# Two interleaved streams of matrix products on one core: runs of second products in place of single ones

## The chip, the core and the metric

The kernel runs on one core of one Trainium2 chip. The metric is device time in microseconds; before the change the median of three runs is 1249.38 us (1248.95 to 1249.69). Engines are named as in the profile: PE is the matrix engine, PEld its weight load, DVE the vector engine, ACT the scalar engine, POOL the GpSimd engine, SP the engine that issues DMAs.

## What is computed

A block-sparse attention (4 batches, 8 heads, 768 tokens, head size 64) feeds a mixture of four dense experts over all 3072 tokens, each with a hidden layer of 1024:

```python
attn = softmax(mask(q @ k.T / 8)) @ v          # mask: window, first and last block, 3 sampled blocks
x = attn.transpose(0, 2, 1, 3).reshape(3072, 512)
p = domain_probs / domain_probs.sum(-1)
for e in range(4):
    h = relu(x @ w1[e])                        # 512 -> 1024: the "first" product
    out += p[:, e:e+1] * (h @ w2[e])           # 1024 -> 512: the "second" product
```

## The kernel before, in words

The expert layers take most of the time, and PE does them as two interleaved streams of work.

A **first product** (line 746, or 725 in the first two sets; written F here) is six matmuls of 128x384: a high part and a low part of weights and tokens (hi*hi, lo*hi, hi*lo) for two slices of 256 inputs, with 384 tokens as columns. In the last three of the five sets seven such products (numbered 2, 1, 5, 6, 3, 7, 4, in that order) stand in for eight, so that their sums are combined on ACT and DVE. Products 2, 5 and 3 are written to the PSUM tile `v`, the others are summed in the PSUM tile `w`; each tile has one buffer, so that a reader on ACT or DVE (`p`, `u`, `z`, `hh`, `hl` at lines 753 to 781) has to be done before PE writes it again. ACT then makes `hh` (ReLU, rounded), and DVE `hl` (the rest).

A **second product** (line 795, written S here) is three matmuls of 128x512 (hh*h2, hh*l2, hl*h2) for one tile of 128 tokens. Three token tiles j = 0, 1, 2 make up 384 tokens; four hidden tiles f = 0 to 3 are summed in the PSUM tile `po`, one buffer for each j. After f = 3 DVE adds `po` times the token's weight to `oacc` (line 810; the "evacuation"), and then f = 0 of the next group may write that buffer.

The function `experts` sets the order of the two streams by counting. It is a generator that emits one product at a time: p counts the first products that are out, q the second ones. Second product q becomes due when p has reached `lead[q]`, which spreads the second products evenly over the first ones at a distance of 10 (`OFF`). Each set of the last three has 8 chunks of 14 first and 24 second products; each of the first two sets has 8 chunks of 8 and 12. One more rule (`wait`) puts a second product ahead of first product 4, since 7 and 4 write `w` one after the other with a reader between them. With every first product the casts of a later weight tile are emitted as well: a copy on ACT (line 674), a difference on POOL (line 675), and, for 2, 1, 5 and 6, a sum or difference of raw weights on DVE (lines 678 to 684). `split_w2` (lines 698 and 699) does the same for `w2` after the last use of a tile.

The attention of the next batch is laid between the products by `drive`, which goes by the modelled time of what has been emitted: blocks of score matmuls (L347, L480), transposes (L385, L502) and value products (L416, L531), some of them only right after a second product (`drive(..., 2)`). All engines' queues are in program order. The order is fixed when the program is built.

Of the kernel before, what the change touches and what calls it, by code (L numbers as in the profile page):

```python
# [23 lines left out]
def attention_moe_kernel(ctx: ExitStack, tc, qb, kb, vr, sampled, sampled_t, probs, w1, w2, out):  # L24
# [193 lines left out]
    one = const.tile([1, 1], F32, name="one")  # L218
# [8 lines left out]
    lead = p1.tile([NR, G], F32, name="lead")  # L227
# [392 lines left out]
    def convert(b, r):  # L620
        if b in todo and todo[b][0][0] <= r:
            step(b)

    def need(b, n):
        while b in todo and any(m == n for _, _, m in todo[b]):
            step(b)
# [5 lines left out]
    def plain(m):  # L632
        return m < 2
# [80 lines left out]
    def first(b, c, s, n):  # L714
        ps_m, cp, hp = later["m"], later["c"], later["h"]
        w = wo.pop((b, c, s, n))
        if plain(b):
# [10 lines left out]
            if k == 1:  # L728
                f = 2 * s + i
                ring = int((c * FT + f + FT) % (NH[0] + NH[1]) >= NH[0])  # L730
                hh = hp.tile([P, HS], F32R, name=f"hh{ring}", bufs=NH[ring])
                hl = hp.tile([P, HS], F32R, name=f"hl{ring}", bufs=NH[ring])
                src = W[s]
# [16 lines left out]
        def finish(half, g, src):  # L750
            hh = hp.tile([P, HS], F32R, name=f"hh{g}", bufs=NH[g])
            hl = hp.tile([P, HS], F32R, name=f"hl{g}", bufs=NH[g])
            nc.scalar.activation(hh, src, AF.Relu)
            defer.append(lambda: nc.vector.scalar_tensor_tensor(hl, src, 0.0, f32(hh), op0=ALU.max,  # L754
                                                                op1=ALU.subtract))
            hs[c, 2 * s + half, g] = (hh, hl)
# [30 lines left out]
    def second(b, c, g, f, j):  # L787
        e = c // CPE
        if f == 0:
            po[j] = later["m"].tile([P, DM], F32, name="po", bufs=HS // P)  # L790
        p = po[j]
        (hh, hl), (h2, l2) = hs[c, f, g], w2t[b, c, f]
        js = slice(j * P, (j + 1) * P)
        for n, (a, w) in enumerate(((hh, h2), (hh, l2), (hl, h2))):
            nc.tensor.matmul(p, a[:, js], w, start=f == 0 and n == 0,  # L795
                             stop=f == FT - 1 and n == 2)
        if j == HS // P - 1:
            hs.pop((c, f, g))
            if g == 0 or plain(b):
                w2t.pop((b, c, f))  # L800
                split_w2((b * NCH + c + 1) * FT + f)
        if f < FT - 1:
            return
        tok = (b * HS if plain(b) else (b - 1) * S + g * HS) // P + j
        pe = pr[:, tok, e:e + 1]
        if c == 0:
            accs[tok] = later["o"].tile([P, DM], F32, name="oacc")
            nc.vector.tensor_scalar(accs[tok], p, pe, None, op0=ALU.mult)
        else:
            nc.vector.scalar_tensor_tensor(accs[tok], p, pe, accs[tok], op0=ALU.mult, op1=ALU.add)  # L810
        if c == NCH - 1:
            acc, row = accs.pop(tok), tok * P
            if b < 2:
                row += BLOCK
                if row + P > S:
                    nc.sync.dma_start(out[:BLOCK, :], acc[S - row:, :])
                nc.sync.dma_start(out[row:min(row + P, S), :], acc[:min(P, S - row), :])
            else:
                nc.sync.dma_start(out[row:row + P, :], acc)
# [2 lines left out]
    TB = NCH * (len(ORDER) * T1 + KT * FT * T2)  # L822
    TP = NCH * (len(PLAIN) * T1 + KT // 2 * FT * T2)
    OFF = 10
    NH = (5, 3)

    def experts():

        sets = []
        ends = [0]  # L830
        for b in range(SETS):
            sets.append(([(b, c, s, n) for c in range(NCH) for s, n in (PLAIN if plain(b) else ORDER)],
                         [(b, c, g, f, j) for c in range(NCH) for g in ((0,) if plain(b) else (1, 0))
                          for f in range(FT) for j in range(HS // P)]))
            ends.append(ends[-1] + len(sets[-1][0]))
        one = [x for a, _ in sets for x in a]
        two = [x for _, a in sets for x in a]

        lead = [ends[b] + i * len(a) / len(t) + OFF for b, (a, t) in enumerate(sets) for i in range(len(t))]

        def ready(p):

            q = 0
            for b, (a, t) in enumerate(sets):
                q += min(max(p - OFF + 1 - ends[b], 0), len(a)) * len(t) // len(a)
            return q

        p = q = 0
        after_first = False
        while q < len(two):  # L850

            left = defer[:]
            defer.clear()
            wait = after_first and p < len(one) and one[p][3] == 4 and q < ready(p)
            if wait or p >= min(len(one), lead[q]):
                second(*two[q])
                q += 1
                after_first = False
                took = T2, 2
            else:  # L860
                need(one[p][0], one[p][3])
                first(*one[p])
                p += 1
                after_first = True
                took = T1, 1
            for op in left:
                op()
            for b in todo:
                if p - ends[b] >= EARLY:
                    convert(b, p - ends[b])  # L870
                    break
            yield took

    stream = experts()
    done = [0.0]

# [238 lines left out]
```

## Time and profile before

| | us |
|---|---|
| median of three runs | 1249.38 |
| the profiled execution's own time | 1256.33 |
| its span, first to last instruction | 1254.6 |
| PE busy | 1228.3 (98%) |
| DVE busy | 759.5 (61%) |
| ACT busy | 675.6 (54%) |
| POOL busy | 715.1 (57%) |
| granted clock of PE, mean over the span | 0.997 |

The profiled execution is 7 us longer than the median. PE's busy time uses ends that are modelled, and a matmul's record overlaps the next one's; the distance from one start to the next is what tells the cost of a matmul here, so the timeline of PE's starts is the view to read. Rows of the timeline give start, duration, engine, line, operation and tiles; matmuls of one name in a row are merged with their count.

### The profile page before, as it was taken

How to read it: one execution, taken by the hardware profiler on the slowest of the kernel's cores; microseconds unless marked ns; L12 is line 12 of the kernel's file. 1: busy time of each engine (PE TensorE's matmuls, PEld its weight loads, DVE VectorE, ACT ScalarE, POOL GpSimd, SP SyncE). 2: the span in 40 equal slices, each digit the busy share in tenths (PEclk: the TensorE clock that was granted, in tenths of full speed). 3: DMA queues.
4: the chain of work that ended last, by engine and by line, in shares of the span. 5: the costliest groups of instructions: out<-in, count | busy, mean ns of one | idle time of the engine just before them, and what ended most of it. 6: DMA issues, size and time to landing. Idle time of an engine off the chain costs nothing.

```text
span 1254.6 us, 29430 instructions
## 1 busy us (share of the span) xinstructions
PE 1228.3 (98%) x11028; PEld 1051.0 (84%) x11028; DVE 759.5 (61%) x1743; ACT 675.6 (54%) x1817; POOL 715.1 (57%) x846
## 2 busy tenths in 40 slices
PE   5899999999999999999999999999999999999998
PEld 3688888878888888888888888888888888888887
DVE  5455536545448676656658676666756855555553
ACT  4556645666656446666665445666664544444441
POOL 5566656666659646555546664556544855555551
PEclk9899999999999999999999999999999999999999
DMA  8556646585635425444413442444431222222211
GB/s 242 159 184 172 192 167 214 181 233 183 189 104 196 152 77 153 151 126 124 131 60 131 160 125 84 138 153 135 142 91 47 89 97 66 67 70 68 66 51 54
DMA packets 75051, 163.84 MB, mean 131 GB/s; under 512 B 8923, under 2 KB 20188, under 8 KB 74908
## 3 DMA queue, kind: packets, MB, share of 16 engines
q1 hardware_dynamic: 69238, 144.65, 36.8%
q0 software_dynamic: 5632, 17.31, 5.0%
q8 instruction: 87, 1.43, 0.5%
q14 instruction: 56, 0.46, 0.1%
q10 hardware_dynamic: 38, 0.00, 0.0%
HBM read 155.63 MB, written 6.29 MB: 129 GB/s over the span
## 4 chain that ended last, share of the span: by engine, by line
PE 67%; DVE 2%; issue 0%; POOL 0%; POOLq 0%; DVEq 0%
PE po L795 32%; PE w L746 16%; PE v L746 12%; PE s L347 2%; PE o L416 2%; PE tp L385 1%; DVE oacc L810 1%; PE ow L531 1%; PE sw L480 1%; PE tw L502 0%; DVE d L597 0%; DVE hl L754 0%; DVE r L682 0%; PE w L725 0%; PE v L725 0%
## 5 line engine op out<-in xcount | busy, mean ns | idle before, releaser
L675 POOL TENSOR_TENSOR wo<-r,wo 128x256 fp32r<-128x256 f32 x288 | 241.2, 840 | 278.5 <-ACT wo L674 275.0
L795 PE MATMUL po<-h,hh 128*128 128x512 f32 x768 | 307.4, 400 | 1.4 <-DVE oacc L810 1.4
L795 PE MATMUL po<-h,hl 128*128 128x512 f32 x768 | 304.5, 397 | 0.0
L795 PE MATMUL po<-l,hh 128*128 128x512 f32 x768 | 303.5, 395 | 0.1
L746 PE MATMUL w<-xo,wo 128*128 128x384 f32 x1152 | 233.2, 337 | 0.2 <-DVE u L776 0.2
L699 POOL TENSOR_TENSOR l<-r,h 128x512 fp32r<-128x512 f32 x160 | 211.2, 1320 | 37.6 <-ACT h L698 36.9
L746 PEld LDWEIGHTS w<-xo,wo 128*128 128x128 f32 x1152 | 205.4, 188 | 19.2 <-DVE z L781 0.8
L746 PE MATMUL v<-xo,wo 128*128 128x384 f32 x864 | 176.1, 338 | 0.0
L795 PEld LDWEIGHTS po<-h,hl 128*128 128x128 f32 x768 | 143.8, 187 | 31.6 <-issue 0.3
L746 PEld LDWEIGHTS v<-xo,wo 128*128 128x128 f32 x864 | 154.6, 188 | 13.0 <-ACT z L773 0.2
L661 POOL TENSOR_TENSOR wo<-r,wo 128x256 fp32r<-128x256 f32 x128 | 95.8, 750 | 116.4 <-ACT wo L660 109.2
L795 PEld LDWEIGHTS po<-h,hh 128*128 128x128 f32 x768 | 144.2, 188 | 20.4 <-DVE oacc L810 2.8
L795 PEld LDWEIGHTS po<-l,hh 128*128 128x128 f32 x768 | 144.2, 188 | 12.4
L674 ACT CAST wo<-r 128x256 fp32r<-128x256 f32 x288 | 114.3, 397 | 49.1 <-PE w L746 31.3
L810 DVE SCALAR_TENSOR_TENSOR oacc<-po,pr,oacc 128x512 f32<-128x512 f32 x168 | 124.1, 741 | 24.1 <-PE po L795 24.0
L374 ACT ACTIVATE p<-p,mx 128x256 f32<-128x256 f32 (+1 forms) x192 | 95.4, 498 | 69.6 <-DVE mx L371 69.6
L698 ACT CAST h<-r 128x512 fp32r<-128x512 f32 x160 | 99.0, 619 | 11.5 <-PE po L795 11.3
L212 POOL DMA_INDIRECT v<-in_vr_dram,vidx x88 | 85.1, 967 | 26.6 <-issue 18.4
L371 DVE CUSTOM_DVE_ANT_1 p<-s,mask 128x256 f32<-128x256 f32 (+1 forms) x192 | 69.8, 418 | 49.1 <-PE s L347 38.6
L725 PE MATMUL w<-xo,wo 128*128 128x384 f32 x384 | 80.5, 342 | 1.1 <-issue 1.0
L725 PE MATMUL v<-xo,wo 128*128 128x384 f32 x384 | 78.4, 340 | 0.5 <-ACT xo L322 0.5
L769 DVE TENSOR_TENSOR p<-w,p 128x384 f32<-128x384 f32 x48 | 26.7, 555 | 84.8 <-PE w L746 81.6
(148 smaller groups left out, 1666.7 us busy)
## 6 DMA issues: line engine op xcount, KB each, us to landing
r<-in_w_dram SPq DMA_DIRECT2D x80, 512.0 KB
r<-in_w_dram SPq DMA_DIRECT2D x160, 256.0 KB
v<-in_vr_dram SPq DMA_DIRECT2D x44, 384.0 KB
kr<-in_kb_dram SPq DMA_DIRECT2D x76, 192.0 KB
k<-in_kb_dram SPq DMA_DIRECT2D x8, 768.0 KB
v<-in_vr_dram SPq DMA_DIRECT2D x12, 512.0 KB
out_dram<-oacc SPq DMA_DIRECT2D x23, 256.0 KB
q<-in_qb_dram SPq DMA_DIRECT2D x20, 256.0 KB
```

Of the source, the lines that this page charges most:

```text
L212: nc.gpsimd.indirect_dma_start(out=v[:G, i, 1], out_offset=None, in_=vr, element_offset=b * S * DM, in_offset=bass.IndirectOffsetOnAxis(ap ...
L371: nc.vector.tensor_tensor_reduce(p.rearrange("p (a b) -> p a b", b=BLOCK), s[h][:n, i], mk, -SCALE, 3.0e38, ALU.add, ALU.min, mx[:n])
L374: nc.scalar.activation(p, p, AF.Exp, bias=mx[:n], scale=-1.0, accum_out=self.sums[:n, m:m + 1])
L661: nc.gpsimd.tensor_sub(o[:, 1], r[s][:, i, k], f32(o[:, 0]))
L674: nc.scalar.copy(o[:, 0], src)
L675: nc.gpsimd.tensor_sub(o[:, 1], src, f32(o[:, 0]))
L698: nc.scalar.copy(h, r)
L699: nc.gpsimd.tensor_sub(l, r, f32(h))
L725: nc.tensor.matmul(W[s], w[:, wi, t], x[xi][:, k * KH + t], start=k == 0 and m == 0, stop=k == 1 and m == 3 * KH - 1)
L746: nc.tensor.matmul(ps, w[:, wi, t], x[:, xi, t], start=fresh and m == 0, stop=m == 3 * KH - 1, skip_group_check=not fresh)
L795: nc.tensor.matmul(p, a[:, js], w, start=f == 0 and n == 0, stop=f == FT - 1 and n == 2)
L810: nc.vector.scalar_tensor_tensor(accs[tok], p, pe, accs[tok], op0=ALU.mult, op1=ALU.add)
```

## The change

The loop in `experts` is given a counter `burst`. Where no run is under way, it looks whether the next three second products are all due (`RUN = 3`; fewer at the very end); if so it begins a run of them. If they are not, and the next first product is 4 and the last one was a first product, it begins a run of those that become due with that product, three at most. During a run only second products are emitted.

```diff
+    RUN = 3
...
-        p = q = 0
+        p = q = burst = 0
         after_first = False
         while q < len(two):
             left = defer[:]
             defer.clear()
-            wait = after_first and p < len(one) and one[p][3] == 4 and q < ready(p)
-            if wait or p >= min(len(one), lead[q]):
+            if not burst:
+                due = sum(1 for n in range(q, min(q + RUN, len(two))) if p >= min(len(one), lead[n]))
+                if due == min(RUN, len(two) - q):
+                    burst = due
+                elif after_first and p < len(one) and one[p][3] == 4:
+                    burst = min(RUN, ready(p) - q)
+            if burst:
+                burst -= 1
                 second(*two[q])
                 q += 1
                 after_first = False
```

The number of instructions is the same. In the built program, apart from the last 18 second products, which stand in a row in both, the 750 others stood in 158 runs of one and 296 runs of two, with one first product between two runs. They now stand in 250 runs of three, with one first product (48 times) or two (202 times) between them. The first run begins after 12 first products in place of 10. A run of three is j = 0, 1, 2 of one hidden tile.

PE in the last but one chunk of the last set, from first product 1 up to 6, around the second products f = 3 of the group `hh1`, whose results are evacuated. Before (`xo1`, `xo5`, `xo6` are the tokens' side of products 1, 5 and 6; `po` has one number for each j):

```order
L746 MATMUL w_16182<-xo1_14205,wo_16046 128x384 x6
L795 MATMUL po_16082<-h2_16075,hh1_16131 128x512
L795 MATMUL po_16082<-l2_16076,hh1_16131 128x512
L795 MATMUL po_16082<-h2_16075,hl1_16132 128x512
L795 MATMUL po_16098<-h2_16075,hh1_16131 128x512
L795 MATMUL po_16098<-l2_16076,hh1_16131 128x512
L795 MATMUL po_16098<-h2_16075,hl1_16132 128x512
L746 MATMUL v_16206<-xo5_14234,wo_16068 128x384 x6
L795 MATMUL po_16116<-h2_16075,hh1_16131 128x512
L795 MATMUL po_16116<-l2_16076,hh1_16131 128x512
L795 MATMUL po_16116<-h2_16075,hl1_16132 128x512
```

PE at the same place after the change:

```order
L746 MATMUL w_16182<-xo1_14201,wo_16046 128x384 x6
L746 MATMUL v_16197<-xo5_14230,wo_16059 128x384 x6
L795 MATMUL po_16108<-h2_16075,hh1_16128 128x512
L795 MATMUL po_16108<-l2_16076,hh1_16128 128x512
L795 MATMUL po_16108<-h2_16075,hl1_16129 128x512
L795 MATMUL po_16113<-h2_16075,hh1_16128 128x512
L795 MATMUL po_16113<-l2_16076,hh1_16128 128x512
L795 MATMUL po_16113<-h2_16075,hl1_16129 128x512
L795 MATMUL po_16117<-h2_16075,hh1_16128 128x512
L795 MATMUL po_16117<-l2_16076,hh1_16128 128x512
L795 MATMUL po_16117<-h2_16075,hl1_16129 128x512
```

First product 5 has moved ahead of the second products for j = 0 and 1; after them 6 and 3 follow as a pair, and then f = 0, j = 0 of the next group.

DVE at this place, from the sum of product 1 (`p`) to that of product 6 (`u`). Before:

```order
L769 TENSOR_TENSOR p_16169<-w,p_16169 128x384
L680 TENSOR_TENSOR r_16003<-r_16003 128x256
L810 SCALAR_TENSOR_TENSOR oacc<-po,pr,oacc 128x512
L754 SCALAR_TENSOR_TENSOR hl_16191<-p_16169,hh_16190 128x384
L810 SCALAR_TENSOR_TENSOR oacc<-po,pr,oacc 128x512
L682 TENSOR_TENSOR r_16003<-s_16171,r_16003 128x256
L810 SCALAR_TENSOR_TENSOR oacc<-po,pr,oacc 128x512
L776 TENSOR_TENSOR u_16233<-w,z_16213 128x384
```

After:

```order
L769 TENSOR_TENSOR p_16165<-w,p_16165 128x384
L680 TENSOR_TENSOR r_16003<-r_16003 128x256
L682 TENSOR_TENSOR r_16003<-s_16167,r_16003 128x256
L754 SCALAR_TENSOR_TENSOR hl_16191<-p_16165,hh_16190 128x384
L810 SCALAR_TENSOR_TENSOR oacc<-po,pr,oacc 128x512 x3
L776 TENSOR_TENSOR u_16229<-w,z_16204 128x384
```

The three evacuations now stand in one piece, all of them behind the weight difference of line 682 (which waits for POOL) and behind `hl`; before, only the third stood behind line 682.

## Prediction

> **What bounds the kernel now.** I read the page first, then the chain of work that ended last, then PE's waits, and then the timeline of PE's starts. In the page, the span and PE's row; of the chain, its shares by engine; of PE's waits, the only one that lies in the stream of products and exceeds a microsecond:
>
> ```profile
> span 1254.6 us, 29430 instructions
> PE 1228.3 (98%) x11028; PEld 1051.0 (84%) x11028; DVE 759.5 (61%) x1743; ACT 675.6 (54%) x1817; POOL 715.1 (57%) x846
> ...
> PE 67%; DVE 2%; issue 0%; POOL 0%; POOLq 0%; DVEq 0%
> ...
> PE po L795 <- DVE oacc L810: 1.4, 3, 0.5
> ```
>
> PE is busy 98% of the span, the chain runs through it, and it waits for others hardly at all. So the time is the sum of the distances between PE's starts, and a change in the order of products is worth what it changes in these distances, less any wait that it makes. The next view is PE's timeline in the last set, which has no attention; each row below opens a product or a run (second products have three rows each, only the first is shown).
>
> ```profile
> 1115.96 1.21 PE L746 MATMUL w<-xo,wo 128*128 128x384 f32 x6
> 1117.00 0.39 PE L795 MATMUL po<-h,hh 128*128 128x512 f32 x1
> ...
> 1118.39 1.21 PE L746 MATMUL v<-xo,wo 128*128 128x384 f32 x6
> 1119.43 0.39 PE L795 MATMUL po<-h,hh 128*128 128x512 f32 x1
> ...
> 1121.87 0.39 PE L795 MATMUL po<-h,hh 128*128 128x512 f32 x1
> ...
> 1122.57 1.22 PE L746 MATMUL v<-xo,wo 128*128 128x384 f32 x6
> 1123.63 0.39 PE L795 MATMUL po<-h,hh 128*128 128x512 f32 x1
> ...
> 1147.33 1.21 PE L746 MATMUL w<-xo,wo 128*128 128x384 f32 x6
> ```
>
> From 1115.96 to 1147.33 is one chunk, 14 first and 24 second products: 31.37 us. Inside it a run of two S takes 1118.39 - 1117.00 = 1.39, and the F behind it 1.04 (1119.43 - 1118.39). A single S takes 1122.57 - 1121.87 = 0.70, and the F behind it 1.06 (1123.63 - 1122.57). With 10 runs of two and 4 of one, and 1.045 for the F behind a run of two, this gives 10 x 2.435 + 4 x 1.76 = 31.39: the pieces account for the chunk.
>
> Now the same products where nothing alternates: the last second products of the program, behind the last F, and the first F of the program.
>
> ```profile
> 1237.26 1.21 PE L746 MATMUL w<-xo,wo 128*128 128x384 f32 x6
> 1238.30 0.39 PE L795 MATMUL po<-h,hh 128*128 128x512 f32 x1
> ...
> 1239.00 0.39 PE L795 MATMUL po<-h,hh 128*128 128x512 f32 x1
> ...
> 1239.69 0.39 PE L795 MATMUL po<-h,hh 128*128 128x512 f32 x1
> ...
> 1240.38 0.39 PE L795 MATMUL po<-h,hh 128*128 128x512 f32 x1
> ...
> 1249.22 0.39 PE L795 MATMUL po<-h,hh 128*128 128x512 f32 x1
> ```
>
> ```profile
> 54.93 2.24 PE L725 MATMUL w<-xo,wo 128*128 128x384 f32 x12
> 57.01 2.24 PE L725 MATMUL v<-xo,wo 128*128 128x384 f32 x12
> ...
> 63.25 0.39 PE L795 MATMUL po<-h,hh 128*128 128x512 f32 x1
> ```
>
> Behind an F, three S take 0.70, 0.69 and 0.69, 2.08 in all (1238.30 to 1240.38). The 13 S from 1240.38 to 1249.22 take 0.680 each. Eight F in a row (54.93 to 63.25) take 1.040 each. So an S that follows an F soon costs 0.01 to 0.02 more than one in a long row, and an F behind a single S 0.02 more than one behind an F. Alternating costs a little at every turn. That is the cost which longer runs can lower.
>
> **The change, part by part.** No instruction is added or removed; 454 runs of S become 250.
>
> The products themselves. In a chunk of the last three sets, 8 runs of three and 14 F: 8 x 2.08 + 14 x 1.04 = 31.20, against 31.37: 0.17 less, and for 24 such chunks 4.1. In a chunk of the first two sets, 4 runs of one and 4 of two become 4 of three, with 8 F: before 4 x 1.76 + 4 x 2.435 = 16.78, after 4 x 2.08 + 8 x 1.04 = 16.64: 0.14 less, and for 16 chunks 2.2. Together 6.3. In 8% of the runs an attention block stands at the edge (231 of the 250 runs follow an F directly), so I take 92%: **-5.8 us**.
>
> Two values in this are not shown by the trace as such. The third S of a run that an F follows: at least 0.68 (the long row), at most 0.70 (a single S); I take 0.69, the one third S there is. Over 250 runs that is 2.5 either way. The F behind a run of three: at least 1.04 (behind an F), at most 1.06 (behind a single S); it falls from 1.06 to 1.045 with the second S, so I take 1.04. The high end adds 0.02 x 250 = 5.0. All low ends give 0.92 x (-6.3 - 2.5) = -8.1; all high ends 0.92 x (-6.3 + 7.5) = +1.1.
>
> The Trainium skill, on the page "TensorE: Matmul & The Clock Gate", section "Back-to-back issue gap", gives the distance of matmuls from their own columns alone, N/2.4 + 2.5 ns; by it the order of products could not change PE's time and this sum would be nil. The rows above disagree: equal matmuls of 512 columns stand 0.680/3 = 0.227 us apart in a long row and 0.70/3 = 0.233 behind an F.
>
> Attention blocks. A block costs more behind an S than behind an F, and a product more behind a block:
>
> ```profile
> 610.37 0.40 PE L795 MATMUL po<-h,hl 128*128 128x512 f32 x1
> 610.70 1.09 PE L347 MATMUL s<-kr,q 64*32 64x256 f32 x32
> ...
> 612.75 0.50 PE L795 MATMUL po<-h,hh 128*128 128x512 f32 x1
> ...
> 613.55 1.23 PE L746 MATMUL w<-xo,wo 128*128 128x384 f32 x6
> ...
> 620.20 1.21 PE L746 MATMUL w<-xo,wo 128*128 128x384 f32 x6
> 621.24 1.03 PE L385 MATMUL tp<-ident,p 128*128 128x128 f32 x8
> ```
>
> The last matmul of an S takes 0.33 before a block (610.37 to 610.70), 0.10 over the usual 0.23; an F before a block takes its 1.04 (620.20 to 621.24). Behind a block the S takes 0.80 (612.75 to 613.55), 0.10 over. In the new order 89 blocks follow an S in place of 87, so +0.2; the returns cost the same kind of 0.1 for F and S. I take 0, with 1 us either way.
>
> The waits. F next to F brings no write of `v` or `w` nearer to the next one than one F and three S in between (1.04 + 2.08 = 3.12 us of PE work, the shortest before as well); between 7 and 4 there are now three S, 2.08, in place of two, 1.39. The one chain that is rearranged is the evacuation: all three now stand behind line 682, which waits for POOL's weight difference of product 1. Its pieces, in the quiet set:
>
> ```profile
> 1117.27 0.56 DVE L769 TENSOR_TENSOR p<-w,p 128x384 f32<-128x384 f32 x1 [2.38 <-PE w L746]
> 1117.74 0.41 DVE L680 TENSOR_TENSOR r<-r 128x256 f32<-128x256 f32 x1
> 1117.86 0.53 ACT L753 ACTIVATE hh<-p 128x384 fp32r<-128x384 f32 x1 [2.26 <-DVE p L769]
> ...
> 1118.29 0.39 ACT L674 CAST wo<-r 128x256 fp32r<-128x256 f32 x1
> ...
> 1118.74 0.55 DVE L754 SCALAR_TENSOR_TENSOR hl<-p,hh 128x384 fp32r<-128x384 f32 x1
> ...
> 1119.20 0.74 DVE L810 SCALAR_TENSOR_TENSOR oacc<-po,pr,oacc 128x512 f32<-128x512 f32 x1
> ```
>
> Counted from the start of F 1 (1115.96): ACT's cast ends at 2.72, POOL's difference takes 0.74 (the 527.41 row below) and ends near 3.5. Then on DVE line 682 (0.41, as line 680), `hl` (0.55) and the first evacuation (0.74): done at 5.2, or near 6.0 if POOL's next 0.74 comes in between. PE comes back to j = 0 after F 1, F 5, three S, F 6 and F 3: 4 x 1.04 + 2.08 = 6.24. It fits, by 0.2 to 1.0. The second and third evacuation need 0.74 each while PE needs 0.70 for each S; they keep up. Where POOL is full, line 682 takes longer:
>
> ```profile
> 527.41 0.74 POOL L675 TENSOR_TENSOR wo<-r,wo 128x256 fp32r<-128x256 f32 x1
> 528.11 0.73 POOL L675 TENSOR_TENSOR wo<-s,wo 128x256 fp32r<-128x256 f32 x1
> 528.19 2.19 DVE L682 TENSOR_TENSOR r<-s,r 128x256 f32<-128x256 f32 x1 [2.28 <-POOL wo L675]
> ...
> 530.30 0.74 DVE L810 SCALAR_TENSOR_TENSOR oacc<-po,pr,oacc 128x512 f32<-128x512 f32 x1
> ...
> 531.10 0.50 PE L795 MATMUL po<-h,hh 128*128 128x512 f32 x1 [0.47 <-DVE oacc L810]
> ```
>
> Here it took 2.19 while POOL worked without a pause, and PE waited for the third evacuation. The Trainium skill, page "SBUF — State Buffer", section "Who interferes with whom", says that a DVE instruction with two SBUF inputs contends with GpSimd's reads for a shared port; the trace agrees, 2.19 against 0.41. With 2.19 in the chain above the first evacuation ends at 3.5 + 2.19 + 0.55 + 0.74 = 7.0, 0.8 late, unless an attention block stands in between. The three waits of before (1.4 us) may go, and a few of 0.8 may come where a set begins or POOL gathers: from -1.4 to 4 x 0.8 = +3.2. I take 0, near the middle.
>
> The sum is -5.8, against the profiled execution's own span of 1254.6 (1248.8 after) and its own time of 1256.33. The median of the runs is 7 us lower than that, and I move it by the same amount: 1249.38 - 5.8 = **1243.6**.
>
> **The rivals.** *The turns cost the same per S, however long the run.* A third S of 0.70 and 1.06 for the F behind it, all high ends: +1.1, 1250.5, no change that can be told. For it: only one row shows a third S behind an F. Against it: the F falls from 1.06 to 1.045 already behind two.
>
> *Only the columns count.* Then the sum is nil and the time stays at 1249.4. The rows of 0.680 and 0.70 speak against it. The rule of the Trainium skill cited above amounts to this.
>
> *The evacuations hold PE up: slower.* If line 682 is held by POOL in many places, each costs 0.8 and 0.1 for the restart (the waiting matmul took 0.50, others 0.39). From (5.8 + 2.5)/0.9 = 9 places on it is slower than before by 2.5. With half of the 32 such places in the two sets that carry both attention and this chain it is 16 x 0.9 = 14.4: 1249.38 + 8.6 = 1258.0. For it: all three evacuations stand behind line 682 now. Against it: two more F stand between the run and j = 0, and the chain fits in the quiet set.
>
> *More than forecast.* A third S of 0.68, and the three waits gone: -8.1 - 1.4, 1239.9. For it: the long row shows 0.68, though only from the fourth S on.
>
> **How the numbers follow.** The forecast, from -3 to -8, has 0.64; more than forecast 0.12; the turns 0.09; only the columns 0.08; the evacuations 0.07. A change of 0.2%, 2.5 us, is about what can be told from none. Faster: the first two, 0.76. Same: the next two, 0.17. Slower: 0.07. The range runs from 1240.6, most of the way to the fourth rival, to 1247.4, where a few new waits or part of a high end eat two thirds of the gain; the two rivals without change and the slower one stay outside.
>
> **What would show it.** In the new timeline of the last set a chunk should take 31.20 (31.1 to 31.3), a run of three 2.08, an F behind it 1.04, and the second F of a pair 1.04. PE's waits for line 810 should stay under 4 us in all, with none in the last set. Chunks of 31.35 or more would show the turns rival; waits for `oacc` in ten places or more the slower one. I would be wrong, above all, if the F behind three S costs 1.06.

## The result, and the profile after

The changed kernel takes **1268.29 us** (median of 4 runs, 1267.27 to 1269.39); the kernel before, on the same chip, 1249.54 (4 runs, 1248.95 to 1250.85). The ratio is 1.0149, 95% interval 1.0137 to 1.0162: 18.7 us slower. The forecast was 1243.6, with a range up to 1247.4.

The page of the changed kernel, its profiled execution (1267.27 us): the span and the busy times, and the chain's shares by engine.

```profile
span 1265.6 us, 29436 instructions
PE 1228.0 (97%) x11028; PEld 1052.1 (83%) x11028; DVE 755.2 (60%) x1743; ACT 676.6 (53%) x1817; POOL 704.7 (56%) x846
...
PE 85%; DVE 7%; issue 2%; POOL 2%; ACT 2%; DMA 2%; DVEq 0%; SPq 0%; ACTq 0%; POOLq 0%
```

The work is the same, and PE is busy for as long as before (1228.0 against 1228.3). The chain now runs through DVE for 7% in place of 2%. So time came in as waiting. PE's waits name the places; in each row stand the time in all, how many times, and the longest:

```profile
PE tp L385 <- DVE p L400: 6.2, 4, 2.6
PE po L795 <- DVE oacc L810: 4.9, 6, 1.3
...
PE w L746 <- DVE z L781: 2.2, 4, 0.9
...
PE w L746 <- DVE hl L754: 1.2, 2, 0.6
```

Inside the stream of products and attention blocks PE waits 6.2 + 4.9 + 2.2 + 1.2 = 14.5 us for DVE, where it waited 1.4 before. The largest row is for line 400, which the prediction does not mention: the scaling of the attention weights, half of which DVE does in the first two batches.

The trace of before came from an execution that was 7 us long, so I also counted without its beginning and end: from the first F to the last product, as the sum of the distances between PE's starts. Before takes 1197.3 us, after 1212.3, so 15.0 more. Of this the attention blocks hold 6.4 (157.3 against 150.9). Products that stand more than 0.15 us over their steady distance (1.040 for an F, 0.680 for an S) hold 8.6 (their excess is 15.2 against 6.5). And the small excess of all other products, in which the turns lie, holds nothing: 35.7 in both. The gain that was forecast is not there, and waits came on top of it.

First the turns. PE's timeline in the last set after the change; each row opens a product or a run of three S:

```profile
1126.71 1.23 PE L746 MATMUL w<-xo,wo 128*128 128x384 f32 x6
1127.78 1.20 PE L746 MATMUL v<-xo,wo 128*128 128x384 f32 x6
1128.82 0.39 PE L795 MATMUL po<-h,hh 128*128 128x512 f32 x1
...
1130.90 1.23 PE L746 MATMUL w<-xo,wo 128*128 128x384 f32 x6
1131.96 1.20 PE L746 MATMUL v<-xo,wo 128*128 128x384 f32 x6
1133.00 0.39 PE L795 MATMUL po<-h,hh 128*128 128x512 f32 x1
...
1158.12 1.23 PE L746 MATMUL w<-xo,wo 128*128 128x384 f32 x6
```

Three S take 2.08 (1128.82 to 1130.90), as forecast. The second F of a pair takes 1.04, as forecast. But the F behind the three takes 1.06 to 1.07 (1130.90 to 1131.96, 1126.71 to 1127.78), not 1.04. The median over the trace is 1.066. A chunk, from 1126.71 to 1158.12, takes 31.41; before it took 31.37.

Then the waits. The first kind, at an evacuation (the first row is F 1, the second and third are gathers that POOL issues for the attention):

```profile
603.18 1.23 PE L746 MATMUL w<-xo,wo 128*128 128x384 f32 x6
...
605.51 0.93 POOL L212 DMA_INDIRECT v<-in_vr_dram,vidx  x1
...
606.75 0.92 POOL L212 DMA_INDIRECT v<-in_vr_dram,vidx  x1 [0.30 <-issue]
...
607.69 0.75 POOL L675 TENSOR_TENSOR wo<-r,wo 128x256 fp32r<-128x256 f32 x1
...
608.39 0.74 POOL L675 TENSOR_TENSOR wo<-s,wo 128x256 fp32r<-128x256 f32 x1
608.47 2.19 DVE L682 TENSOR_TENSOR r<-s,r 128x256 f32<-128x256 f32 x1 [2.83 <-POOL wo L675]
609.08 1.28 POOL L699 TENSOR_TENSOR l<-r,h 128x512 fp32r<-128x512 f32 x1
...
610.58 0.55 DVE L754 SCALAR_TENSOR_TENSOR hl<-p,hh 128x384 fp32r<-128x384 f32 x1
...
611.05 2.06 DVE L810 SCALAR_TENSOR_TENSOR oacc<-po,pr,oacc 128x512 f32<-128x512 f32 x3
...
611.85 0.50 PE L795 MATMUL po<-h,hh 128*128 128x512 f32 x1 [1.34 <-DVE oacc L810]
```

Line 682 waits 2.83 for POOL, then takes 2.19 while POOL goes on from line 675 to line 699 without a pause. `hl` and all three evacuations stand behind it, and PE waits 1.34 for the first of them. This is the mechanism of the slower rival, at two places (here and at 916.25, 1.33), which make 2.7 of the 4.9 us. The other four waits for `oacc` (0.35, 0.74 and twice 0.59) and the two for `hl` lie around the starts of the sets. There the chain on DVE also holds a difference of the tokens' conversion (line 594 or 597), which takes 1.97 to 2.05 beside POOL.

The second kind, at an attention block in the second set:

```profile
246.49 5.00 DVE L400 TENSOR_SCALAR p<-p,rec 128x256 f32<-128x256 f32 x1
...
246.75 1.31 POOL L699 TENSOR_TENSOR l<-r,h 128x512 fp32r<-128x512 f32 x1
...
248.01 1.43 POOL L661 TENSOR_TENSOR wo<-r,wo 128x256 fp32r<-128x256 f32 x2
...
249.41 1.25 POOL L699 TENSOR_TENSOR l<-r,h 128x512 fp32r<-128x512 f32 x1
...
250.63 0.71 POOL L661 TENSOR_TENSOR wo<-r,wo 128x256 fp32r<-128x256 f32 x1
...
251.64 1.81 PE L385 MATMUL tp<-ident,p 128*128 128x128 f32 x8 [2.24 <-DVE p L400]
...
253.11 2.27 PE L725 MATMUL w<-xo,wo 128*128 128x384 f32 x6
```

One DVE instruction of 128x256 takes 5.00 us, and ends, at 251.49, just after POOL has come through five differences in a row (250.63 + 0.71 = 251.34). PE's transposes wait 2.24 for it, and then run slowly: eight take 1.47 (251.64 to 253.11) where they took 0.79 at 607.36 to 608.15, and the F behind them 2.06 in place of 1.06. The granted clock of that stretch, from the view by windows (last three columns: clock, DMA share, GB/s):

```profile
250.00:256.00 6.00, 4.26 (x17) 3.94 (x18) 2.29 (x4) 1.76 (x4) 1.34 (x2) 0.72 0.80 242
256.00:262.00 6.00, 6.00 (x117) 4.78 (x116) 3.53 (x14) 3.09 (x11) 3.30 (x4) 1.00 0.38 119
```

How far the hold spreads, from the view of single lines (shortest, median, longest in ns). Before, lines 400 and 682:

```profile
L400 DVE TENSOR_SCALAR p<-p,rec x36: 336/403/1195, 110.3 to 362.8; 128x256 f32<-128x256 f32 x28, 64x256 f32<-64x256 f32 x8
L682 DVE TENSOR_TENSOR r<-s,r x48: 374/420/2194, 383.2 to 1214.0; 128x256 f32<-128x256 f32 x48
  POOL wo L675: 7.3, 5
```

After:

```profile
L400 DVE TENSOR_SCALAR p<-p,rec x36: 335/353/5000, 107.3 to 364.2; 128x256 f32<-128x256 f32 x28, 64x256 f32<-64x256 f32 x8
L682 DVE TENSOR_TENSOR r<-s,r x48: 425/945/2189, 380.3 to 1224.5; 128x256 f32<-128x256 f32 x48
  POOL wo L675: 62.3, 47
```

Line 682 now waits for POOL 47 times out of 48 (5 times before) and is typically held too: its median goes from 420 to 945 ns. But the long holds are not new: it took 2.2 us four times before and takes it twice now. What is new is that the evacuations stand behind it. Line 400 is as quick as before at most places and held at a few, and there for longer (5000 ns in place of 1195).

### The profile page after: what moved, and what is told of

It is laid out like the page before. It is cut to its first block, busy times and chain, and to the rows that moved or that the text cites. A ratio compares the mean times of both kernels' runs of the same rounds, so it can differ in the third digit from the quotient of the medians.

```text
span 1265.6 us, 29436 instructions
## 1 busy us (share of the span) xinstructions
PE 1228.0 (97%) x11028; PEld 1052.1 (83%) x11028; DVE 755.2 (60%) x1743; ACT 676.6 (53%) x1817; POOL 704.7 (56%) x846
## 4 chain that ended last, share of the span: by engine, by line
PE 85%; DVE 7%; issue 2%; POOL 2%; ACT 2%; DMA 2%; DVEq 0%; SPq 0%; ACTq 0%; POOLq 0%
PE po L795 38%; PE w L746 15%; PE v L746 11%; PE v L725 5%; PE w L725 5%; PE o L416 3%; PE s L347 3%; PE tp L385 3%; DVE oacc L810 1%; PE sw L480 1%; DMA r<-in_w_dram 1%; DVE p L400 1%; POOL wo L675 1%; POOL l L699 1%; PE ow L531 1%
## 5 line engine op out<-in xcount | busy, mean ns | idle before, releaser
L675 POOL TENSOR_TENSOR wo<-r,wo 128x256 fp32r<-128x256 f32 x288 | 232.6, 811 | 279.4 <-ACT wo L674 273.1
L699 POOL TENSOR_TENSOR l<-r,h 128x512 fp32r<-128x512 f32 x160 | 214.1, 1338 | 164.1 <-ACT h L698 153.7
L746 PE MATMUL w<-xo,wo 128*128 128x384 f32 x1152 | 236.6, 340 | 3.3 <-DVE z L781 2.2
L746 PE MATMUL v<-xo,wo 128*128 128x384 f32 x864 | 173.6, 335 | 0.0
L810 DVE SCALAR_TENSOR_TENSOR oacc<-po,pr,oacc 128x512 f32<-128x512 f32 x168 | 118.1, 738 | 26.7 <-PE po L795 26.5
L661 POOL TENSOR_TENSOR wo<-r,wo 128x256 fp32r<-128x256 f32 x128 | 94.2, 745 | 49.8 <-ACT wo L660 49.7
L682 DVE TENSOR_TENSOR r<-s,r 128x256 f32<-128x256 f32 x48 | 41.9, 872 | 62.3 <-POOL wo L675 62.3
L753 ACT ACTIVATE hh<-u 128x384 fp32r<-128x384 f32 x48 | 25.2, 524 | 94.3 <-DVE u L778 93.9
```

The source lines that it names most:

```text
L661: nc.gpsimd.tensor_sub(o[:, 1], r[s][:, i, k], f32(o[:, 0]))
L675: nc.gpsimd.tensor_sub(o[:, 1], src, f32(o[:, 0]))
L699: nc.gpsimd.tensor_sub(l, r, f32(h))
L746: nc.tensor.matmul(ps, w[:, wi, t], x[:, xi, t], start=fresh and m == 0, stop=m == 3 * KH - 1, skip_group_check=not fresh)
```

## The experiments

The theory after this reading: DVE is held up by POOL at two kinds of place, line 682 ahead of the evacuations and line 400 ahead of the transposes, and that is the loss; the turns bring nothing for runs of three. The rivals: the longer runs themselves cost time at the turns, or the order of DVE's queue alone makes the waits and POOL has no part.

The medians of the kernel before were 1249.17, 1256.06, 1255.28 and 1249.09 us in the four groups of experiments below, so the groups are compared by ratios; 0.001 is 1.25 us.

### The kernel before, again (no edit)

> The kernel before, unchanged, profiled once more. Its first profile took 1256.33 us, 7 us over the median of its runs; the changed kernel's took 1267.27, within 1 us of its median. If the first profile was an accident (its first product began at 52.6 us, the changed kernel's at 48.5), this one spans about 1247 to 1249 us with the first product near 48.5, and the loss in the stretch of products is about 18 us. If the profile itself slows the old order, the span is about 1254 again and the loss between the traces is 15 us from the first product on.

1251.88 us in its one profiled run, span 1250.2. PE's waits are as in the first trace, 1.3 us in 3 for `oacc`, and one of 0.4 for line 400; 1195.5 us from the first F to the last product, 1.8 less than in the first trace, so that the changed kernel's loss in this stretch is 16.8 against this trace. So the picture of before stands, and the differences named above belong to the change.

### Line 682 behind the evacuations

```diff
-                        nc.vector.tensor_sub(a11, s1[s], a11)
+                        late.append(lambda a=a11, t=s1[s]: nc.vector.tensor_sub(a, t, a))
...
+    late = []
     def first(b, c, s, n):
+        while late:
+            late.pop(0)()
```

The weight difference is emitted just ahead of the next F, and so behind the run of S and its evacuations.

> The changed kernel with one DVE instruction moved: the weight difference of line 682 is emitted just before the next first product, so that it stands behind the three evacuations and not ahead of them. Theory A (the evacuations come late because line 682 waits for POOL ahead of them): PE's waits for the evacuation (4.9 us idle, about 7 with the restarts of 0.1 and the slower first matmuls) go, and the time falls to about 1261 to 1262. Rival T (the loss is the price of the turns between first and second products): nothing changes, 1268 within 1. Rival B (POOL's longer unbroken work slows whatever DVE does with two operands or copies in SBUF): the wait moves to another reader, 1265 to 1268.

1257.48 us (4 runs), ratio 1.0063 [1.0045, 1.0080]: 10.8 less than the changed kernel. PE's waits in this kernel:

```profile
PE tp L385 <- DVE p L400: 6.6, 5, 2.6
...
PE w L750 <- DVE z L785: 2.1, 2, 1.1
...
PE po L799 <- DVE oacc L814: 0.5, 1, 0.5
```

The wait for the evacuations falls from 4.9 to 0.5, that for `hl` from 1.2 to 0.5, and line 400's stays. More came back than these 5.1 us of waits, and more than the 6 to 7 us expected. By distances between PE's starts the gain is 9.3: 7.1 in products far over their steady distance, 1.4 in attention blocks, 0.8 in small excess. So a wait costs more than its own row: the matmuls behind it are late as well.

### Line 400's work on ACT

```diff
-            if m % 2 or self.b > 1:
+            if True:
                 nc.scalar.mul(p, p, self.rec[:n, m:m + 1])
```

> The changed kernel with the scaling of the attention's weights (line 400, on DVE in the first two batches) done on ACT as in the later batches. Theory B (DVE's copy-like work in SBUF is held while POOL works without a pause; line 400 took 5.0 us at 246.5 in place of 0.3 to 0.6): PE's waits for it (6.2 us idle in 4 places, and 3.4 us at half clock after the longest) go, 1260 to 1262. Theory T: 1268. If ACT becomes late by its 36 more instructions of 0.5 us: 1268 or more, with waits for ACT.

1260.98 us (4 runs), ratio 1.0088 [1.0071, 1.0105]: 7.3 less than the changed kernel. Here it is the other row that stays:

```profile
PE po L795 <- DVE oacc L810: 4.9, 6, 1.3
...
PE tp L385 <- ACT p L398: 1.3, 3, 0.6
```

### Both edits

> Both edits together. If A and B are both right and apart from each other, the gains add: about 13 to 14 us, 1254 to 1255. If they are one cause that only moves, clearly less than the sum: over 1259. Theory T: 1268. What then remains over the 1249.5 of the kernel before is for the waits for z and hl (lines 781 and 754, 3.4 us idle) and the turns.

1251.21 us (10 runs), ratio 1.0014 [1.0005, 1.0024]: 17.1 less than the changed kernel, where the two alone make 10.8 + 7.3 = 18.1. The expectation, 1254 to 1255, was too high because line 682 alone had given more than expected. So the two edits take back nearly all of the loss, and their gains nearly add up. What stays in the stream, with one wait of 0.6 for `hl`:

```profile
PE w L750 <- DVE z L785: 2.1, 2, 1.0
...
PE tp L385 <- ACT p L398: 1.3, 3, 0.6
...
PE po L799 <- DVE oacc L814: 0.5, 1, 0.5
```

With 4.5 us of waits left, and with runs of three, the kernel is no faster than the kernel before. Its small excess is 35.2 in place of 35.7: the turns of runs of three are worth next to nothing, as the timeline says.

### Both edits in the kernel before

> The kernel before with both edits of the run before this one (line 682 behind the evacuations, the scaling of line 400 on ACT) and no runs of three. If the edits only mend what the runs of three broke, they are worth what the old order loses at these places: 1.3 us of waits for the evacuation and 0.4 for line 400, with restarts 2 to 3 us: 1246.5 to 1247.5. If they are gains of their own as large as in the new order (17 us), 1232.

Ratio 0.9991 [0.9982, 1.0000] (11 runs), about 1 us, less than the 2 to 3 expected; there was little to remove. Runs of three with the same edits are 2.9 us behind it (1.0014 against 0.9991).

### Runs of two

```diff
-    RUN = 3
+    RUN = 2
```

> The changed kernel with RUN = 2 in place of 3: 375 runs of two, with one first product between them 297 times and two 78 times. The turns, by the rows of before (1.39 for a run of two, 1.045 for the first product behind it, 1.04 for the next): a chunk 12 x 2.435 + 2 x 1.04 = 31.30, 0.07 under 31.37, and in the first two sets 6 x 2.435 + 2 x 1.04 = 16.69 against 16.78; over all about 3 us less than before, 1246 to 1247, if no waits are added. If POOL's work is held together by any pair of first products, waits for lines 810, 781 and 400 come back: 1252 to 1260.

Ratio 1.0098 [1.0084, 1.0113] (5 runs), about 12 us more, where 3 to 11 were expected for the case with waits. Its timeline in the last set:

```profile
1131.12 1.21 PE L746 MATMUL v<-xo,wo 128*128 128x384 f32 x6
1132.16 0.39 PE L795 MATMUL po<-h,hh 128*128 128x512 f32 x1
...
1133.55 1.21 PE L746 MATMUL w<-xo,wo 128*128 128x384 f32 x6
1134.59 0.39 PE L795 MATMUL po<-h,hh 128*128 128x512 f32 x1
```

Two S take 1.39 and the F behind them 1.04. Over the whole trace the small excess is 33.2 us in place of 35.7: turns can be saved, but by runs of two, not of three. The waits take it back, and more: 6.4 us in 8 for `oacc`, 4.5 for `z`, 3.0 for `hl`.

### Runs of two with both edits

> RUN = 2 with both edits. If turns and waits are the two separate terms they seem to be: 3 us from the turns and 2 to 3 from the waits of before, 1243.5 to 1245. If runs of two give nothing: 1247 as the edits alone.

Ratio 1.0126 [1.0111, 1.0142] (4 runs): no better than without the edits. The small excess is low again (33.3), but the waits are still there (`z` 5.1 us, `oacc` 3.9, `hl` 3.0), all around the starts of the sets, where the tokens' conversions stand in DVE's queue.

### Runs of six

```diff
-    RUN = 3
+    RUN = 6
```

> RUN = 6: 125 runs of six, with three or four first products between them, to read the distances in longer runs (its waits are many and its time is no matter: 1275 or more, since three first products in a row leave the readers of v and w 1.04 us). If the slower matmuls are a matter of the first nine behind a turn, a run of six takes 2.08 + 3 x 0.680 = 4.12, the first product behind it 1.06 to 1.07, the others 1.04. If they go on with the run, 4.15 or more.

1301.55 us in one run, against 1256.06 for the kernel before in this group. Its fourth to sixth S take 0.680 each, and the F behind six 1.066 (medians), as behind three. So the F does not get dearer beyond three, and the S get cheaper from the fourth on. The waits bury it: `hl` alone holds PE for 14.9 us in 17.

### The changed kernel without the low part of w2

Line 699, POOL's 160 differences `l2`, is left out; a tile of zeros stands in their place, and PE multiplies by it in the same order.

```diff
-        l = wp.tile([P, DM], F32R, name="l2")
+        l = zero[0]
         nc.scalar.copy(h, r)
-        nc.gpsimd.tensor_sub(l, r, f32(h))
```

> The changed kernel with the low part of w2 left out: POOL's 160 differences of line 699 (214.1 us in all) are not computed, a tile of zeros stands in their place, and PE's work and order stay as they are. Its output is therefore less exact. Theory (DVE instructions are held while POOL works without a pause, and line 682 waits for POOL): line 682's mean falls from 872 ns to under 650, line 400's from 820 to under 650, PE's waits for oacc from 4.9 us to under 2 and those for line 400 from 6.2 to under 2; the time falls by 10 to 17 us, to 0.999 to 1.007 of the kernel before. Rival (the order of DVE's queue alone makes the waits, POOL has no part): the means of lines 682 and 400 and the time stay within 3 us of the changed kernel, ratio 1.013 or more.

Ratio 1.0005 [0.9995, 1.0015] (10 runs): 1.0149 - 1.0005 is 18.0 us less than the changed kernel, where 10 to 17 were expected. Lines 400 and 682 in this kernel:

```profile
L400 DVE TENSOR_SCALAR p<-p,rec x36: 334/350/895, 111.0 to 363.1; 128x256 f32<-128x256 f32 x28, 64x256 f32<-64x256 f32 x8
L682 DVE TENSOR_TENSOR r<-s,r x48: 424/938/949, 378.9 to 1214.5; 128x256 f32<-128x256 f32 x48
```

```profile
PE w L748 <- DVE z L783: 2.1, 4, 0.9
...
PE po L797 <- DVE oacc L812: 1.2, 2, 0.6
...
PE tp L385 <- DVE p L400: 0.6, 1, 0.6
```

The longest line 400 falls from 5000 to 895 ns, the longest line 682 from 2189 to 949. The waits for both fall from 11.1 to 1.8 us. The median of line 682 stays at 938, its mean is 778, not under 650 as expected: POOL's line 675 beside it still holds it for one instruction, and that PE does not feel. The waits for `z` are as before the omission; in the trace of the changed kernel they stand behind other DVE work (at 479.08 PE waits 0.89 for a `z` that follows six transposes of 1.44 in all), not behind a held instruction.

### The control: the kernel before without the low part of w2

> The same omission in the kernel before, as the control: the same 160 POOL differences left out, the low part of w2 zero. Theory: there were hardly any waits to remove, so the time falls by 0 to 4 us, ratio 0.997 to 1.000. Rival (POOL's work costs time everywhere, whatever the order, or zeros in the operand change PE's speed): it falls by as much as the changed kernel does, 10 us or more.

Ratio 0.9966 [0.9954, 0.9977] (7 runs): 4.2 us less, just over the 0 to 4 expected. The same omission gives 18.0 in the new order and 4.2 in the old one. So 13.8 of the 18.7 us are what POOL's 160 differences cost in the new order beyond the old one. The rival of DVE's order alone falls for that part.

### The conversions later, and earlier

What runs of two still wait for, and most of what runs of three still wait for, lies around the set starts, so the tokens' conversions there were moved, with both edits in place:

```diff
-    EARLY = -8
+    EARLY = -5
```

Runs of two:

> Runs of two with both edits, and the token conversions at the start of a set begun 5 first products ahead of it in place of 8 (so that the three DVE differences of 128x768, 1.4 to 2.0 us each, no longer fall between the evacuations of the chunk before). Theory (the waits left at the set starts come from these differences in DVE's queue): PE's waits for oacc and z fall from 9 us to under 3, the time to 0.998 to 1.003 of the kernel before, and if the turns' 2.6 us stay won, under it. Rival (the conversions are then too late for the first products of the set): new waits of PE for xo at the set starts, ratio 1.010 or more.

Ratio 1.0078 [1.0060, 1.0096] (4 runs), down from 1.0126. Waits for `oacc` fall to 1.6 us, those for `hl` to 0.2, but those for `z` only to 3.7, and new ones of 1.6 for `xo` and 1.2 for ACT's cast of line 674 appear. That lies between the theory (at most 1.003) and the rival (1.010 or more). Runs of three:

> Runs of three with both edits, and the conversions begun 5 first products ahead in place of 8. Theory: the waits for z and oacc that were left at the set starts (2.1 and 0.7 us) go, ratio 0.999 to 1.001. Rival (conversions too late): new waits for xo, ratio 1.003 or more.

Ratio 1.0144 [1.0126, 1.0161] (4 runs), up from 1.0014: 7.2 us of waits for `z` in two places and 2.6 for `oacc`. At both places `z` stands on DVE behind a difference of the conversion (line 594) that waits 1.2 us for ACT's cast and then takes 2.0. No wait for `xo` appears, which the rival had named.

With -12 in place of -5, runs of two, runs of three, and the kernel before:

> Runs of two with both edits and the conversions begun 12 first products ahead of a set in place of 8, so that the three DVE differences of 128x768 stand clear of the evacuations of the two last chunks. Theory (these differences in front of the evacuations make the waits): PE's waits for oacc fall from 3.9 us to under 2, the half-clock stretches behind them go, ratio 1.002 to 1.008. Rival (the conversions' work as such, the products' needs at the set start): 1.010 or more.

> Runs of three with both edits and the conversions begun 12 ahead. Theory: ratio 0.998 to 1.001, oacc and z waits under 2 us together. Rival: 1.003 or more, as the waits only change place.

> The kernel before with both edits and the conversions begun 12 ahead, the control. Either theory: 0.997 to 1.000, since there are hardly any waits at its set starts.

Runs of two 1.0093 [1.0076, 1.0110], runs of three 1.0029 [1.0018, 1.0041], the kernel before 0.9992 [0.9983, 1.0002]. With runs of two the waits for `z` and `oacc` keep their size (5.1 and 4.0 us); those for `hl`, 3.0 us, go. This does not decide about the theory, because the edit moved the three differences at two of the three set starts only. Ahead of the third set they begin after the same first products with -8 and with -12, and the longest wait for `oacc` still comes right behind the last of them:

```profile
372.62 2.04 DVE L597 TENSOR_TENSOR d<-xr 128x768 f32<-128x768 f32 x1
...
375.38 0.51 PE L799 MATMUL po<-h,hh 128*128 128x512 f32 x1 [2.07 <-DVE oacc L814]
```

At the two later sets, where they did move, the waits for `hl` (1.49 each) are gone. The waits for `z` there (2.6 each) stand behind another part of the conversion, a difference of line 594 that waits for ACT's cast and that this edit does not move. So the conversions stand ahead of the long waits in DVE's queue, but no run took all of them away: that they are the cause with runs of two is argued, not shown. With runs of three `z` waits 3.3 us and `oacc` 0.5, against the theory's less than 2 together. No order with longer runs beat the kernel before.

## Why the prediction was wrong

**The turns, -5.8: wrong in one term.** The step was "it falls from 1.06 to 1.045 with the second S, so I take 1.04" for the F behind a run of three. It measures 1.066. Three S at 2.08 and the second F of a pair at 1.04 were right. A chunk is then 8 x 2.08 + 8 x 1.066 + 6 x 1.04 = 31.41, as measured, where 31.20 was forecast and 31.37 stood before. The prediction had named the high end, 1.06, as what would make it wrong above all, and gave it 0.09: two points, behind one S and behind two, were drawn on as a falling line, and nothing in the trace of before showed a run of three with an F behind it. Runs of two show that the saving exists (2.5 us by the trace), at the length that most of the old runs already had.

**The waits, 0 within -1.4 to +3.2: wrong, and this decides the sign.** 14.5 us of waits in place of 1.4. Two things failed. The first is the chain to the first evacuation: "It fits, by 0.2 to 1.0" was worked out in the quiet set, where indeed no such wait came. With a hold of 2.19 the prediction let it end 7.0 us after the start of F 1, and took four places of 0.8, "where a set begins or POOL gathers". Those were the places, but there were six, of 0.35 to 1.34. At the one shown above the chain ended after 8.6 (603.18 to 611.79): POOL's difference, which was to end near 3.5, ended at 5.3 (607.69 + 0.75 - 603.18), because two gathers of the attention stood ahead of it in POOL's queue. An attention block gave PE only part of that time back, and it waited 1.34. At the set starts the evacuations and `hl` stand behind the conversions, which are not in the prediction's chain. In all it came to 4.9 us for `oacc` and 1.2 for `hl`, and moving line 682 gave 10.8 back. The second is that line 400 was not looked at, because no product waits for it: its hold gave 6.2 us of waits, a slow stretch of PE behind one of them, and 7.3 us when it was moved.

The rule to see it was at hand. The same section of the Trainium skill that the prediction cites, page "SBUF — State Buffer", "Who interferes with whom", counts the tensor-with-scalar operation among those that can take the port shared with GpSimd, and says that whoever issues first blocks the other for the whole instruction. The trace agrees that line 400 is held, 5.00 us against a median of 0.35, but not with the rest: it was held across five POOL differences, not one, and had begun at 246.49, ahead of the first of them (246.75).

**The attention blocks, 0 within 1: wrong.** They hold 6.4 us more, all of it in the transposes of line 385 (39.8 against 33.4), and 4.0 of it are waits for line 400 inside a block. The blocks' edges were costed, not what the blocks wait for.

**The slower rival, 0.07: right in its mechanism, not in its count.** It named line 682 held by POOL with the evacuations behind it, and 9 places or more. There were 6 waits for `oacc`, none in the last set, and only two of them behind a held line 682. Its 1258.0 lies nearer to the result than the forecast, for part of the reason: the waits for line 400 and the conversions are not in it.

**What stays open.** Why line 400 meets longer rows of POOL's differences. In the first two sets, where it runs, POOL came through three or more differences without a pause (less than 0.1 us between them) 21 times in place of 12, but in the last three sets 34 times in place of 46; so for line 682 the rows are not more, only what stands behind it is new. One lead, not tested: POOL's line 699 sat idle for 164.1 us ahead of its differences in place of 37.6, mostly for ACT's cast of `w2`. It is also open what makes the waits at the set starts with runs of two, and why an F behind three or six S costs as much as behind one, while behind two it does not. It is not a matter of the tile: behind two S the F takes 1.044 for every j, and for `v` as for `w` (traces of before and of runs of two).

## What to carry to other kernels

When a reordering moves no work, look first at every in-order queue for instructions that another engine can hold, and at who waits behind each, also in the stages that the change does not name; the quiet stage shows the steady cost, not the waits. A pitch that is known for runs of one and two is not known for three: give both ends their weight, or forecast no change. And when one engine runs on without a pause, count what its neighbours lose: here one omission of its work was worth 4 us in one order and 18 in the other.

## What was not expected of the hardware

The distance of an S depends on its place in the run: 0.698, 0.691, 0.692 for the first three behind an F, 0.680 from the fourth on (medians, runs of three and of six). The F behind the run takes 1.062, 1.044, 1.066, 1.066 behind one, two, three and six S, against 1.040 behind an F: not a falling row. The cause was not found.

A DVE instruction beside POOL shows steps: line 682 takes 0.42 us free, 0.94 beside one POOL difference, 2.19 beside two in a row, and line 400 took 3.70 and 5.00 us where POOL ran through five:

```profile
120.63 3.70 DVE L400 TENSOR_SCALAR p<-p,rec 128x256 f32<-128x256 f32 x1
```

A wait of 2.24 us on PE was followed by a granted clock of 0.72 over the 6 us around it; with 0.68 more in the transposes and 1.00 more in the F behind them, it cost 3.9 us. That is no rule: after the longer wait of 2.62, at 124.48 in the same trace, the clock stayed at 1.00 (122 to 130).
